# GpSimd's share of the first stage from chunk 6 on given to VectorE, and the sum of the flags taken in the second stage

## The chip, the cores and the metric

The kernel runs on one NeuronCore of a Trainium2 chip. Its time is the device time of one execution in microseconds (us), as the median of several runs. In the rows of the profile the engines are called PE (TensorE, with PEld for its weight loads), DVE (VectorE), ACT (ScalarE), POOL (GpSimd) and SP (SyncE, whose queue issues the DMAs).

## The reference

The program is a complex-decay linear attention followed by two feed-forward blocks, all in float32.

```python
def _attn_ref(q, k, v, a_re, a_im):            # (B, H, S, D) = (4, 8, 768, 48)
    mag = np.sqrt(a_re * a_re + a_im * a_im)
    scale = np.minimum(mag, 0.999) / (mag + 1e-06)
    a_re_n, a_im_n = (a_re * scale, a_im * scale)
    for t in range(S):
        ar, ai = (a_re_n[:, :, t, :, None], a_im_n[:, :, t, :, None])
        new_re = ar * S_re - ai * S_im
        new_im = ar * S_im + ai * S_re
        S_re, S_im = (new_re + einsum('bhd,bhe->bhde', k_t, v_t), new_im)
        y[:, :, t] = einsum('bhd,bhde->bhe', q_t, S_re)
    return y

x = attention output as (3072 tokens, 384)
x = (1 / (1 + exp(-(x @ w_gate))) * (x @ w_val)) @ w_out      # d_ff 1536
h = x @ w_in;  out = (h - tanh(h)) @ w_out2                   # d_ff 2048
```

## The kernel before

The 3072 tokens are cut into 24 chunks of 128. For each chunk the decays' angles and magnitudes are computed (functions `theta`, `phase`, `sincos`, `magnitude`), q and k are multiplied by them, and the attention within the chunk and the state passed on to the next are done with small matmuls (`pe_units`). Two chunks make a block of 256 tokens, and the first feed-forward block runs over the 12 blocks, 12 slices of the hidden dimension each: two products on TensorE into a PSUM tile `gv` (line 888), the gate on ScalarE (896) and VectorE (903), the result split into a high and a low part (ScalarE 911, VectorE 912), and three steps later the product back into `acc` (935). That is the first stage; the attention of the chunks to come is woven into it. The second stage (from about 713 us of the span) runs the second feed-forward block over six groups of 512 tokens: `hstep` (1070), `cubic` on ScalarE and VectorE, `split2` (1082, 1083) and `fin` (1096).

Each float32 product that needs it is made of three products of a rounded high part and a difference. The weights of the second block are decoded and split while the first stage runs: `Decoder.tick` (line 289) loads a raw slice, ScalarE and VectorE make the value `sg` (lines 64, 66, 72, 75), `split` (320) lets ScalarE write the high part (323) and the engine in `low` the difference (325), and SyncE stores both in DRAM (327). There are 32 such slices. `low` is POOL alone in the kernel before.

`shared(c, k)` (line 442) says which engine does the elementwise product number `k` of chunk `c`. From chunk 6 on POOL does numbers 9 and 10, k times the inverse suffix of the magnitudes (`suf`, line 566) and q times their running product (`B`, line 567); VectorE does the rest. `suf` comes from a scan on VectorE (549), followed there by `whole` (554, four columns) and the scan for `B` (562). The products feed `stack` (584, 586, 590), and this the scores (716), the transposes of k (728, copied by ScalarE in 729) and the states (781).

Late in the first stage `late_within` tests the decays of the first six chunks again for the flags (424 to 426). `open2` (1017) calls `flag_sum` (978): a maximum over the flags on VectorE (980), a product with a column of ones on TensorE (984), a copy (985). A flag above zero would send the program to a general path; with these inputs it is not taken.

What sets the order: the functions are called in an order given by `merge` and `until`; SyncE's queue keeps that order as written, and the instructions of the other engines are put in order by a scheduler that plans with its own estimates of durations. Each engine then runs its list strictly in order, so an instruction that waits holds all behind it. PSUM tiles come from pools of a few buffers: `pat` with three for the attention, `P2["h"]` with three for `h` in the second stage and `h4` with one more for every fourth step.

Of the kernel before, what the change touches and what calls it, by code (L numbers as in the profile page):

```python
# [8 lines left out]
F32 = mybir.dt.float32  # L9
# [12 lines left out]
NF1, NF2 = FF1 // 128, FF2 // 128  # L22
# [24 lines left out]
POOLED = ((9, 10), (3, 4, 9, 10), (3, 4, 6, 10), (2, 3, 4, 6, 9, 10, 11), (3, 4, 5), (10,))  # L47
# [3 lines left out]
EARLY = 6  # L51
# [192 lines left out]
def kernel(ctx: ExitStack, tc: tile.TileContext, ri, qk, vv, w1, w2, out):  # L244
    nc = tc.nc
    w1i = w1.bitcast(I32)
    w2i = w2.bitcast(I32)
# [18 lines left out]
    pat = att.enter_context(tc.tile_pool(name="pat", bufs=3, space=PSUM, side="right"))  # L266
# [72 lines left out]
    for f in range(NF1):  # L339
        for p in range(2):  # L340
            n = 2 * f + p
# [98 lines left out]
        return load, test  # L440

    def shared(c, k):
        return nc.gpsimd if (k in POOLED[c] if c < EARLY else k in (9, 10)) else nc.vector

    def theta(c):

# [23 lines left out]
        def t2():  # L470
            A, C, R = d["A"], d["C"], d["R"]
            shared(c, 2).tensor_tensor(R, A, C, ALU.add)
# [51 lines left out]
    def magnitude(c):  # L524
# [39 lines left out]
        def m5():  # L564
            Q, K = qkt[c][:, 0], qkt[c][:, 1]
            shared(c, 9).tensor_tensor(K, K, suf, ALU.mult)  # L566
            shared(c, 10).tensor_tensor(Q, Q, d["B"], ALU.mult)
# [376 lines left out]
    def moe1(units, extra):  # L944
# [8 lines left out]
        for n, (j, f, cols) in enumerate(order):  # L953
            if n == last:
                run_to(until[n])
                open2()
            dec1.ready(min(3 * f + 4, 36) if j == 0 and cols is A else 36 if j > 1 else 0)
            gv(n)
            if n >= 1:
                split(n - 1)  # L960
            run_to((until[n] + until[n + 1]) / 2)
            extra(2 * (n - last) + 1)
            if n >= LAG1:
                outp(n - LAG1)
                jo, fo, co = order[n - LAG1]
                if jo == 0 and co is Z:
                    dec1.part(fo, 2, gated[n - 1])
            if n == last - (NB - 3) * NF1 + LAG1:
                early.close()
                gvp[2] = ph1.enter_context(tc.tile_pool(name="pgv2", bufs=1, space=PSUM))  # L970
            gate(n)
            if j == 0 and cols is Z:
                dec1.part(f, 0, gated[n])
                dec1.part(f, 1, gated[n])
            run_to(until[n + 1])
            extra(2 * (n - last) + 2)

    def flag_sum():
        fs = const.tile([RB, 1], F32, name="fs")
        nc.vector.tensor_reduce(fs, flags, mybir.AxisListType.X, ALU.max)  # L980
        one = const.tile([RB, 1], F32, name="one")
        nc.vector.memset(one, 1.0)
        fp = pat.tile([1, 1], F32, tag="at", name="fp")
        nc.tensor.matmul(fp, fs, one)
        nc.vector.tensor_copy(fsum.bitcast(F32), fp)

    with tc.manual_schedule(engines={mybir.EngineType.SP}):
# [27 lines left out]
        P2, W2 = {}, {}  # L1015

        def open2():
            flag_sum()
            att.close()
            P2["x0"] = ph2.enter_context(tc.tile_pool(name="m2x", bufs=1, side="right"))  # L1020
            P2["xr"] = ph2.enter_context(tc.tile_pool(name="m2r", bufs=2, side="right"))
            P2["h"] = ph2.enter_context(tc.tile_pool(name="p2h", bufs=3, space=PSUM, side="right"))
            P2["t"] = ph2.enter_context(tc.tile_pool(name="m2t", bufs=2, side="right"))
            P2["g"] = ph2.enter_context(tc.tile_pool(name="m2g", bufs=3, side="right"))

        w2d = [dram.tile([128, 2, 384], F32, name=f"w2d{s}") for s in range(2 * NF2)]
        dec2 = Decoder(w2i, NF2, 2, ring0, lambda s: 2, (nc.gpsimd,), w2d)

        def load_w2(upto):
            while len(W2) < min(upto, 2 * NF2):  # L1030
                s = len(W2)
                hl = wp.tile([128, 2, 384], F32R, tag=f"w{SLOT[s // 3, s % 3]}", name="whl")
                nc.sync.dma_start(out=hl.bitcast(F32), in_=w2d[s])
                W2[s // 2, s % 2] = hl
# [4 lines left out]
        def load_x2(i, z):  # L1039
            if z == 0:  # L1040
                x2t[i] = P2[f"x{i % 2}"].tile([128, 2, 2, 3, N1], F32R, tag="x2h", name="x2h")
            hl = x2t[i]
            r = P2["xr"].tile([128, 3, N1], F32, tag="x2r", name="x2r")
            nc.sync.dma_start(out=r, in_=x2d[2 * i + z])
            nc.scalar.copy(hl[:, 0, z], r)
            nc.vector.tensor_tensor(hl[:, 1, z], r, hl[:, 0, z].bitcast(F32), ALU.subtract)
# [14 lines left out]
        def hstep(n):  # L1061
            i, f = divmod(n, NF2)
            x = x2t[i]
            ps = P2["h" if n % 4 < 3 else "h4"].tile([128, N2], F32, tag="h", name="h")
            w = W2[f, 0]
            k = 0
            for kt in range(3):
                cs = slice(kt * 128, (kt + 1) * 128)
                for wi, xi in ((0, 0), (0, 1), (1, 0)):
                    nc.tensor.matmul(ps.rearrange("p (z c) -> p z c", z=2), w[:, wi, cs], x[:, xi, :, kt],  # L1070
                                     start=(k == 0), stop=(k == 8))
                    k += 1
            hps[n] = ps

        def cubic(n):
            prev = (lambda: split2(n - 1)) if n else None
            gt2[n] = cubic_rest(nc, P2["t"], hps.pop(n), N2, prev)

        def split2(n):
            g = gt2[n]  # L1080
            gh = P2["g" if n % 4 < 3 else "g4"].tile([128, 2, N2], F32R, tag="gh2", name="gh2")
            nc.scalar.copy(gh[:, 0], g)  # L1082
            nc.vector.tensor_tensor(gh[:, 1], g, gh[:, 0].bitcast(F32), ALU.subtract)  # L1083
            gt2[n] = gh

        def fin(n):
            i, f = divmod(n, NF2)
            gh = gt2.pop(n)
            if f == 0:
                acc2[i] = [P2["acc"].tile([128, DM], F32, tag=f"o{t}", name=f"o{t}") for t in range(4)]  # L1090
            a = acc2[i]
            w = W2[f, 1]
            for t in range(4):
                cs = slice(t * 128, (t + 1) * 128)
                for k, (gi, wi) in enumerate(((0, 0), (0, 1), (1, 0))):
                    nc.tensor.matmul(a[t], gh[:, gi, cs], w[:, wi], start=(f == 0 and k == 0),  # L1096
                                     stop=(f == NF2 - 1 and k == 2), skip_group_check=True)
                if f == NF2 - 1:
                    ob = P2["o"].tile([128, DM], F32, tag="ob", name="ob")
                    if True:  # L1100
                        nc.scalar.copy(ob, a[t])
                    else:
                        nc.vector.tensor_copy(ob, a[t])
                    r0 = i * N2 + t * 128
                    nc.sync.dma_start(out=out[r0:r0 + 128, :], in_=ob)
# [19 lines left out]
        for n in range(LAG2, total + LAG2):  # L1125
            i, f = divmod(n, NF2)
            if n < total:
                load_w2(32)
                hstep(n)
            if n == total:  # L1130
                split2(n - 1)
            if f in (6, 8) and i + 1 < NT // N2:
                load_x2(i + 1, f // 2 - 3)
            if (n - LAG2) % NF2 == NF2 - 1:
                fin(n - LAG2)
            if n < total:
                cubic(n)
            if (n - LAG2) % NF2 != NF2 - 1:
                fin(n - LAG2)
# [66 lines left out]
```

## Time and profile before

| what | value |
|---|---|
| median of 3 runs | 1128.53 us (1127.44 to 1130.26) |
| the profiled execution | 1129.34 us, its span 1127.6 us |
| granted TensorE clock, mean over the span | 0.986 |
| PE busy | 1050.3 us, 93% |
| DVE busy | 885.4 us, 79% |
| ACT busy | 829.3 us, 74% |
| POOL busy | 158.4 us, 14% |
| DMA | 100.21 MB, mean 89 GB/s |

The span is the time from the first to the last instruction; 1.7 us of the execution lie around it. Busy time is the sum of stretches in which the engine had an instruction under way. Between two instructions an engine is idle, and the profile names what ended the idle time. Since all engines run in order, the chain of waits is read from TensorE backwards.

### The profile page before, as it was taken

How to read it: one execution, taken by the hardware profiler on the slowest of the kernel's cores; microseconds unless marked ns; L12 is line 12 of the kernel's file. 1: busy time of each engine (PE TensorE's matmuls, PEld its weight loads, DVE VectorE, ACT ScalarE, POOL GpSimd, SP SyncE). 2: the span in 40 equal slices, each digit the busy share in tenths (PEclk: the TensorE clock that was granted, in tenths of full speed). 3: DMA queues.
4: the chain of work that ended last, by engine and by line, in shares of the span. 5: the costliest groups of instructions: out<-in, count | busy, mean ns of one | idle time of the engine just before them, and what ended most of it. 6: DMA issues, size and time to landing. Idle time of an engine off the chain costs nothing.

```text
span 1127.6 us, 22170 instructions
## 1 busy us (share of the span) xinstructions
PE 1050.3 (93%) x8782; PEld 982.3 (87%) x8782; DVE 885.4 (79%) x1475; ACT 829.3 (74%) x1828; POOL 158.4 (14%) x126
## 2 busy tenths in 40 slices
PE   0597999999999999998999999999999999999996
PEld 0486899899999999997998989999998989999996
DVE  6899885987778798989998743587878788787875
ACT  8698785887878897977988573566767676676764
POOL 2335431011001212122213200000000000000000
PEclk9998999999999999999999999999999999999999
DMA  6356003122112344453344446700101010010000
GB/s 228 129 196 190 29 18 88 36 71 74 46 59 60 129 141 133 136 181 104 124 157 123 154 150 246 259 1 1 56 1 56 1 56 2 1 57 1 28 1 31
DMA packets 36400, 100.21 MB, mean 89 GB/s; under 512 B 4128, under 2 KB 7200, under 8 KB 36288
## 3 DMA queue, kind: packets, MB, share of 16 engines
q1 hardware_dynamic: 36288, 98.71, 26.7%
q8 instruction: 71, 1.16, 0.4%
q14 instruction: 41, 0.34, 0.1%
HBM read 76.68 MB, written 22.02 MB: 88 GB/s over the span
## 4 chain that ended last, share of the span: by engine, by line
PE 64%; DVE 13%; ACT 13%; DMA 6%; issue 3%; POOL 1%; SPq 0%; DVEq 0%; ACTq 0%; POOLq 0%
PE h L1070 18%; PE o L1096 17%; PE gv L888 14%; PE acc L935 7%; DMA ri<-in_ri_dram 3%; DMA raw<-in_w_dram 2%; PE gv L884 2%; PE xps L751 2%; PE sc L716 1%; ACT raw L64 1%; DVE suf L549 1%; ACT raw L66 1%; PE gps L781 1%; DVE gh L912 1%; DVE sg L75 1%
## 5 line engine op out<-in xcount | busy, mean ns | idle before, releaser
L888 PE MATMUL gv<-x,whl 128*128 128x256 f32 x2376 | 314.6, 286 | 3.2 <-ACT x L602 2.6
L888 PEld LDWEIGHTS gv<-x,whl 128*128 128x128 f32 x2376 | 295.4, 192 | 8.4 <-issue 3.4
L1096 PE MATMUL o<-whl,gh 128*128 128x384 f32 x1152 | 216.6, 337 | 0.6 <-ACT gh L1082 0.6
L1070 PE MATMUL h<-x2h,whl 128*128 128x512 f32 x864 | 216.0, 394 | 0.0
L1096 PEld LDWEIGHTS o<-whl,gh 128*128 128x128 f32 x1152 | 203.6, 188 | 9.3 <-ACT gh L1082 0.9
L1070 PEld LDWEIGHTS h<-x2h,whl 128*128 128x128 f32 x864 | 160.9, 188 | 29.9
L935 PE MATMUL acc<-gh,whl 128*128 128x256 f32 x1188 | 174.3, 290 | 2.5 <-DVE gh L912 2.2
L935 PEld LDWEIGHTS acc<-gh,whl 128*128 128x128 f32 x1188 | 153.1, 192 | 7.2 <-DVE gh L912 3.1
L89 ACT ACTIVATE s<-h 128x512 f32<-128x512 f32 x96 | 57.8, 602 | 114.5 <-PE h L1070 114.4
L1083 DVE TENSOR_TENSOR gh<-g,gh 128x512 fp32r<-128x512 f32 x96 | 66.3, 690 | 43.8 <-ACT gh L1082 43.5
L912 DVE TENSOR_TENSOR gh<-g,gh 128x256 fp32r<-128x256 f32 x132 | 73.9, 561 | 30.3 <-ACT gh L911 29.2
L97 DVE TENSOR_TENSOR th<-h,th 128x512 f32<-128x512 f32 x96 | 66.4, 691 | 31.6 <-ACT th L95 30.7
L896 ACT ACTIVATE th<-gv 128x256 f32<-128x256 f32 (+1 forms) x156 | 56.3, 361 | 38.8 <-PE gv L888 30.4
L903 DVE SCALAR_TENSOR_TENSOR g<-th,gv 128x256 f32<-128x256 f32 x132 | 54.3, 413 | 37.8 <-ACT th L896 36.7
L98 DVE COPY_PREDICATED g<-mk,th 128x512 f32<-128x512 int32 x96 | 72.3, 754 | 1.0
L911 ACT CAST gh<-g 128x256 fp32r<-128x256 f32 x132 | 52.8, 401 | 26.2 <-DVE g L903 25.7
L91 DVE SCALAR_TENSOR_TENSOR g<-g,s 128x512 f32<-128x512 f32 x96 | 65.5, 682 | 3.3 <-ACT g L90 3.3
L1082 ACT CAST gh<-g 128x512 fp32r<-128x512 f32 x96 | 59.2, 617 | 11.3 <-DVE g L98 11.0
L92 DVE TENSOR_TENSOR g<-g,h 128x512 f32<-128x512 f32 x96 | 65.0, 678 | 3.1
L566 POOL TENSOR_TENSOR qk<-qk,suf 112x512 f32<-112x512 f32 x21 | 31.2, 1484 | 253.3 <-DMA qk<-in_qk_dram 102.4
L325 POOL TENSOR_TENSOR raw<-sg,raw 128x384 fp32r<-128x384 f32 x32 | 40.6, 1269 | 166.7 <-ACT raw L323 129.1
L96 ACT ACTIVATE mk<-s 128x512 f32<-128x512 f32 x96 | 60.8, 633 | 0.0
(165 smaller groups left out, 1697.5 us busy)
## 6 DMA issues: line engine op xcount, KB each, us to landing
raw<-in_w_dram SPq DMA_DIRECT2D x68, 384.0 KB, 5.1
ri<-in_ri_dram SPq DMA_DIRECT2D x30, 448.0 KB, 5.3
w2d<-raw SPq DMA_DIRECT2D x32, 384.0 KB, 4.1
whl<-w2d SPq DMA_DIRECT2D x32, 384.0 KB, 5.0
qk<-in_qk_dram SPq DMA_DIRECT2D x24, 448.0 KB, 4.9
v<-in_vv_dram SPq DMA_DIRECT2D x24, 320.0 KB, 3.5
x2d<-x SPq DMA_DIRECT2D x12, 384.0 KB, 2.3
x2r<-x2d SPq DMA_DIRECT2D x12, 384.0 KB, 3.7
```

The source lines that it names most:

```text
L91: nc.vector.scalar_tensor_tensor(g, g, TC * TB, s, ALU.add, ALU.mult)
L92: nc.vector.tensor_tensor(g, g, ps, ALU.mult)
L96: nc.scalar.activation(mk, s, AF.Relu, bias=-0.0625)
L97: nc.vector.tensor_tensor(th, ps, th, ALU.subtract)
L98: nc.vector.copy_predicated(g, mk.bitcast(I32), th)
L888: nc.tensor.matmul(ps[:, part], w[:, wi, cs], x[:, xi, kt], start=(k == 0), stop=(k == 8))
L912: nc.vector.tensor_tensor(gh[:, 1], g, gh[:, 0].bitcast(F32), ALU.subtract)
L935: nc.tensor.matmul(o, w[:, wi, cs], gh[:, gi], start=(f == 0 and k == 0 and (m == 0 or m == 2 and not half)), stop=(f == NF1 - 1 and k == ...
L1070: nc.tensor.matmul(ps.rearrange("p (z c) -> p z c", z=2), w[:, wi, cs], x[:, xi, :, kt], start=(k == 0), stop=(k == 8))
L1082: nc.scalar.copy(gh[:, 0], g)
L1083: nc.vector.tensor_tensor(gh[:, 1], g, gh[:, 0].bitcast(F32), ALU.subtract)
L1096: nc.tensor.matmul(a[t], gh[:, gi, cs], w[:, wi], start=(f == 0 and k == 0), stop=(f == NF2 - 1 and k == 2), skip_group_check=True)
```

## The change

There are three edits. `shared` gives the products 9 and 10 of the chunks from 6 on to VectorE. The decoder of the second block's weights takes VectorE for the differences. `flag_sum` is no longer called in `open2` but after the step `n == 16` of the second stage, and its PSUM tile is a piece of a tile of the pool for `h` instead of one of `pat`.

```diff
     def shared(c, k):
-        return nc.gpsimd if (k in POOLED[c] if c < EARLY else k in (9, 10)) else nc.vector
+        return nc.gpsimd if c < EARLY and k in POOLED[c] else nc.vector
...
-        fp = pat.tile([1, 1], F32, tag="at", name="fp")
+        fp = P2["h"].tile([128, 512], F32, tag="h", name="fp")[0:1, 0:1]
         nc.tensor.matmul(fp, fs, one)
         nc.vector.tensor_copy(fsum.bitcast(F32), fp)
...
         def open2():
-            flag_sum()
             att.close()
...
-        dec2 = Decoder(w2i, NF2, 2, ring0, lambda s: 2, (nc.gpsimd,), w2d)
+        dec2 = Decoder(w2i, NF2, 2, ring0, lambda s: 2, (nc.vector,), w2d)
...
                 hstep(n)
+                if n == NF2:
+                    flag_sum()
```

The scheduler makes a new order from this. On VectorE, around the second scan of chunk 19 (in `magnitude`), the list before reads as follows; L590 is the last product of `stack`, for which the scores wait.

```order
L544 SCALAR_TENSOR_TENSOR B<-A,B 112x512
L545 SCALAR_TENSOR_TENSOR A<-C,B 112x512
L549 SCALAR_TENSOR_TENSOR suf<-A,sufs 112x511
L552 RECIPROCAL pseed<-suf 112x4
L554 TENSOR_TENSOR whole_118<-suf,A 112x4
L562 SCALAR_TENSOR_TENSOR B<-A,pseed 112x512
L590 TENSOR_TENSOR qs<-qk,ri 48x4x128
L912 TENSOR_TENSOR gh<-g,gh 128x256
L903 SCALAR_TENSOR_TENSOR g<-th,gv 128x256
```

The same place of VectorE's list in the changed kernel:

```order
L590 TENSOR_TENSOR qs<-qk,ri 48x4x128
L325 TENSOR_TENSOR raw<-sg,raw 128x384
L545 SCALAR_TENSOR_TENSOR A<-C,B 112x512
L912 TENSOR_TENSOR gh<-g,gh 128x256
L903 SCALAR_TENSOR_TENSOR g<-th,gv 128x256
L549 SCALAR_TENSOR_TENSOR suf<-A,sufs 112x511
L552 RECIPROCAL pseed<-suf 112x4
L554 TENSOR_TENSOR whole_118<-suf,A 112x4
L566 TENSOR_TENSOR qk<-qk,suf 112x512
L562 SCALAR_TENSOR_TENSOR B<-A,pseed 112x512
L72 SCALAR_TENSOR_TENSOR sg<-raw 128x384
L912 TENSOR_TENSOR gh<-g,gh 128x256
```

L590 has moved ahead of both scans, a difference L325 stands behind it, the product L566 stands between `whole` and the second scan, and the product L567 is the next row after the last one shown.

On TensorE, where the first block's last slices begin, the list before has the product of the flags between two steps:

```order
L935 MATMUL acc_8304<-gh,whl 128x256 x6
L935 MATMUL acc_8305<-gh,whl 128x256 x3
L984 MATMUL fp<-one,fs 1x1
L888 MATMUL gv<-x,whl 128x256 x18
L935 MATMUL acc_8304<-gh,whl 128x256 x6
```

In the changed kernel that place has no such row, and the product stands in the second stage, after step 16 of `hstep` (L1069 and L1095 are lines 1070 and 1096 of the kernel before):

```order
L1095 MATMUL o_9458<-whl,gh_9832 128x384 x2
L1095 MATMUL o_9459<-whl,gh_9832 128x384 x3
L1069 MATMUL h<-x2h,whl 128x512 x5
L984 MATMUL fp<-one,fs 1x1
L1095 MATMUL o_9456<-whl,gh_9869 128x384 x2
```

It now follows the last of step 16's products instead of the last `acc` products before the new block's `gv`. The maximum over the flags on VectorE (L980) stays where it was.

## Rows read from the trace of the kernel before

**Rows 1.** Waits of TensorE from 160 us on: total us, times, longest.

```profile
PE gps L781 <- ACT kt L729: 6.8, 7, 2.1
PE gv L888 <- ACT x L602: 2.6, 2, 1.4
PE acc L935 <- DVE gh L912: 2.2, 3, 1.5
PE sc L716 <- DVE qs L590: 2.0, 1, 2.0
PE fp L984 <- DVE fs L980: 0.8, 1, 0.8
```

**Rows 2.** Stretches 240:440 and 440:640: length, then PE, PEld, DVE, ACT, POOL busy.

```profile
240.00:440.00 200.00, 200.00 (x2147) 192.75 (x2146) 160.86 (x292) 160.11 (x389) 33.28 (x24) 1.00 0.29 92
...
440.00:640.00 200.00, 189.18 (x2034) 181.77 (x2033) 179.80 (x302) 166.54 (x402) 46.78 (x35) 0.99 0.41 132
```

**Rows 3.** POOL's groups in 440:640: busy us, mean ns, idle before them.

```profile
L325 POOL TENSOR_TENSOR raw<-sg,raw 128x384 fp32r<-128x384 f32 x21 | 26.5, 1262 | 88.7 <-ACT raw L323 68.2 <-DMA qk<-in_qk_dram 13.9 <-issue 5.4
L567 POOL TENSOR_TENSOR qk<-qk,B 112x512 f32<-112x512 f32 x7 | 10.3, 1468 | 4.0 <-DVE B L562 4.0
L566 POOL TENSOR_TENSOR qk<-qk,suf 112x512 f32<-112x512 f32 x7 | 10.3, 1466 | 55.4 <-DMA qk<-in_qk_dram 23.0 <-DVE suf L549 20.4 <-DVE whole L554 11.9
```

**Rows 4.** Three of VectorE's groups in 440:640, same columns.

```profile
L912 DVE TENSOR_TENSOR gh<-g,gh 128x256 fp32r<-128x256 f32 x45 | 29.0, 645 | 6.4 <-ACT gh L911 5.8
L75 DVE SCALAR_TENSOR_TENSOR sg<-raw,sg 128x384 int32<-128x384 int32 x21 | 16.2, 771 | 0.4
L554 DVE TENSOR_TENSOR whole<-suf,A 112x4 f32<-112x4 f32 x7 | 5.3, 753 | 0.0
```

**Rows 5.** Single lines over the whole span: ns min/median/max, first and last start.

```profile
L912 DVE TENSOR_TENSOR gh<-g,gh x132: 389/425/2467, 141.7 to 713.4; 128x256 fp32r<-128x256 f32 x132
L75 DVE SCALAR_TENSOR_TENSOR sg<-raw,sg x32: 544/558/1646, 360.3 to 658.9; 128x384 int32<-128x384 int32 x32
L554 DVE TENSOR_TENSOR whole<-suf,A x24: 127/152/2244, 22.9 to 622.6; 112x4 f32<-112x4 f32 x24
L317 DVE TENSOR_TENSOR whl<-whole,whl x18: 526/554/1455, 82.0 to 171.5; 128x384 fp32r<-128x384 f32 x18
L566 DVE TENSOR_TENSOR qk<-qk,suf x3: 677/682/686, 63.0 to 145.7; 112x512 f32<-112x512 f32 x3
```

**Rows 6.** VectorE in order of time around chunk 19: start, us, instruction.

```profile
512.29 2.24 DVE L554 TENSOR_TENSOR whole<-suf,A 112x4 f32<-112x4 f32 x1
514.46 1.21 DVE L562 TENSOR_TENSOR_SCAN B<-A,pseed 112x512 f32<-112x512 f32 x1
515.70 0.69 DVE L590 TENSOR_TENSOR qs<-qk,ri 48x512 f32<-48x512 f32 x1
516.42 1.38 DVE L912 TENSOR_TENSOR gh<-g,gh 128x256 fp32r<-128x256 f32 x1
```

**Rows 7.** POOL in order of time, same stretch.

```profile
512.24 1.30 POOL L566 TENSOR_TENSOR qk<-qk,suf 112x512 f32<-112x512 f32 x1 [11.09 <-DVE suf L549]
513.50 1.01 POOL L325 TENSOR_TENSOR raw<-sg,raw 128x384 fp32r<-128x384 f32 x1
515.75 1.77 POOL L567 TENSOR_TENSOR qk<-qk,B 112x512 f32<-112x512 f32 x1 [1.23 <-DVE B L562]
```

**Rows 8.** Longest wait of ScalarE in 430:640.

```profile
ACT raw L323 <- DVE sg L75: 11.3, 7, 3.3
```

**Rows 9.** TensorE in order of time where the last block begins.

```profile
671.94 0.19 PE L984 MATMUL fp<-one,fs 112*1 112x1 f32 x2 [0.82 <-DVE fs L980]
673.48 0.38 PE L888 MATMUL gv<-x,whl 128*128 128x256 f32 x1 [1.36 <-ACT x L602]
```

**Rows 10.** SyncE's waits for POOL's differences, whole span.

```profile
SPq L327 <- POOL raw L325: 44.1, 8, 9.8
```

**Rows 11.** ScalarE's first step of `cubic` and what it waited for.

```profile
L89 ACT ACTIVATE s<-h 128x512 f32<-128x512 f32 x96 | 57.8, 602 | 114.5 <-PE h L1070 114.4
```

## The prediction

> **What bounds the kernel now.** I read the page first: PE is busy 93% of the span and carries 64% of the chain that ended last, so only time in which TensorE stands still can be won. Then the waits of TensorE from 160 us on, where the start-up is over: the five largest come to 6.8 + 2.6 + 2.2 + 2.0 + 0.8 = 14.4 us [rows 1]. That is nearly all an edit of this kind can move, 1.3% of the time. The busy times by stretch say where these waits lie: from 240 to 440 us TensorE never pauses (200.00 of 200.00 us) and VectorE is busy 160.86, but from 440 to 640 us, where the decoding of the second block's weights runs as well, VectorE is busy 179.80 and TensorE 189.18, so 10.8 us of its waits are there [rows 2]. The reader is to see that VectorE, with 20.2 us to spare in 200, is the tightest helper in just the stretch where TensorE waits.
>
> Last I read what VectorE does there instruction by instruction. The product for `whole` has four columns and takes 0.15 us in the median, but 2.24 us at 512.29 [rows 5, 6]. It runs exactly while POOL's L566 (1.30 us) and L325 (1.01 us) do, and ends when they end; L912 (median 0.425 us) takes 1.38 us beside POOL's L567 [rows 5 to 7]. So a POOL product holds up the VectorE product that meets it.
>
> One rule bears on the sum. The Trainium skill (SBUF — State Buffer, Who interferes with whom) says that GpSimd and a VectorE instruction with two SBUF inputs compete for one read interface, and the later one stands still until the earlier has finished; the 2.24 us agree with that. If every POOL product in the stretch held VectorE for its whole length, 26.5 + 10.3 + 10.3 = 47.1 us of VectorE's time would come back there [rows 3], and VectorE would have 25.8 us less to do than now; the measured stretch, below, is less than half of this, and the sum goes by it.
>
> **The change part by part.**
>
> *The products given to VectorE.* From 440 to 640 us these are 21 differences L325 and 7 + 7 products of q and k [rows 3]. On VectorE a difference of 128x384 takes 0.55 us (the same form in L317) and a product of 112x512 takes 0.68 us [rows 5]. That adds 21 x 0.55 + 14 x 0.68 = 21.1 us.
>
> *The blocking that goes.* For the three groups that show it most, mean less median, times count [rows 4, 5]: L912 (0.645 - 0.425) x 45 = 9.9; L75 (0.771 - 0.558) x 21 = 4.5; L554 (0.753 - 0.152) x 7 = 4.2. Together 18.6 us, a lower bound, since the smaller groups are left out. VectorE's load therefore becomes at most 179.8 + 21.1 - 18.6 = 182.3 us of 200. As a load the edit is a wash; 17.7 us stay free, and from 240 to 440 us, with 39 us free and no wait of TensorE, the products are hidden whole.
>
> *What the wash is worth to TensorE.* It is not one everywhere. Where POOL's products came in a bunch, they held VectorE for a time the scheduler had not planned. I work one place: around chunk 19 blocking cost 2.24 - 0.15 = 2.1 us in `whole` and 1.38 - 0.43 = 0.95 us in L912 [rows 5, 6]; the new list puts one product (0.68 us) between `whole` and the second scan, and L567 behind L912. Up to L912, that is 3.05 us given back for 0.68 paid. Elsewhere POOL's products met nothing that they could block, and there VectorE now pays in full.
> Term by term:
> - Scores waiting for L590: 2.0 us [rows 1]. L590 stood behind the blocked `whole` and the scan; in the new list it stands ahead of both scans. What is late next there is the mask and then L912, both with less ahead of them. Taken as gone: 2.0 (ends 0 and 2.0; the order decides it).
> - States waiting for ScalarE's copy of the transposed k: 6.8 us in seven waits. ScalarE is late there because it waited itself: 11.3 us in seven waits for VectorE's L75 [rows 8], one of the blocked groups. Bounds 0 (VectorE's load is a wash) and 6.8. I take half, 3.4, since the place worked above gives back more than it pays but the load as a whole does not.
> - `acc` waiting for VectorE's L912: 2.2 us in three, the longest 1.5. L912 is the line with most blocking, but one product now stands ahead of it. Bounds 0 and 2.2; I take 0.8, a third, as only one of the three (after the L912 of 1.38 us) is worked out.
> - `gv` waiting for ScalarE's L602: 2.6 us in two. The one of 1.36 us is at the last block [rows 9]: ScalarE's tests of the flags stand ahead of its L602 and stay there. Of the other 1.2 us I take half, 0.6.
> - The flags' product on TensorE waits 0.82 us, and right after it TensorE waits 1.36 us for L602 [rows 9]. With the product gone it would wait for L602 from the start, so nothing is won: 0, bounds 0 and 0.8 + 0.2.
>
> Against these 2.0 + 3.4 + 0.8 + 0.6 = 6.8 us stands the part of the added load that is not given back, 21.1 - 18.6 = 2.5 us; I put all of it on the path (bounds 0 and 21.1).
>
> *The flags' product in the second stage* costs TensorE 0.2 us there as it did before [rows 9]. Its tile takes one turn of the three buffers for `h`, so step 18 waits for the reading of step 16 instead of step 14. Between the two lie a full step 17 and a row of `fin`, and ScalarE waits 114.4 us in all for `h`, that is, it stands ready when a step ends [rows 11]. Hidden; 1 to 2 us if VectorE is late just there.
>
> *DMAs.* SyncE's list is unchanged, but each store of a slice now waits for VectorE's L325 instead of POOL's, where it waited 44.1 us in all [rows 10]. A later store makes the loads behind it later. POOL's products of q and k mostly waited for their own load [rows 3], so what comes later has some room; I cost it at nothing, and 1 us per place if that cover is gone.
>
> Sum: 6.8 - 2.5 = 4.3 us. From the profiled execution, 1129.34 us, this gives 1125.0; the median of the runs lies 0.8 us under that execution, so the forecast for the median is 1124.2 us. About 3.4 us (0.3%) is what can be told from no change, so the forecast is faster by little more than that.
>
> **The rivals.**
>
> *The wash is a wash (1127.8).* VectorE's time is the same, ScalarE stays late and only the score wait goes. For it: the sum of rows, +21.1 against 18.6, and ScalarE's 166.54 us of 200 are untouched. Against it: the blocking came in bursts. Then 2.0 us are won and half of the 2.5 us lost, so 0.75 us: 1129.34 - 0.8 - 0.75 = 1127.8. The Trainium skill (Perfetto Trace Analysis, Optimizing Scalar/DVE Operations) says of the two engines that, as they share a read port, moving work between them "might not help"; by this the time would be that of before, and the loads in these rows agree with it.
>
> *All waits of the tight stretch go (1116.5).* If the scheduler's plan, in which nothing is blocked, is now kept on the chip, TensorE runs from 440 to 640 as it does from 240 to 440: 6.8 + 2.0 + 2.2 + 1.2 = 12.2 us less, with the extra load in VectorE's 17.7 free us. For it: not one wait where VectorE has 39 us free. Against it: VectorE stays nearly as full as it is.
>
> *VectorE takes over POOL's waits (1133.7).* POOL idled 68.2 us for ScalarE's L323 before the differences and 36.9 us for q and k's load [rows 3]; that cost nothing, as nothing stood behind it. On VectorE the gates L903 and L912 stand behind each such wait. VectorE has 17.7 us left for 35 products, so the point from which it decides is a mean wait of 0.5 us. At 0.65 us, 5.2 us go on the path: 1129.34 - 0.8 + 5.2 = 1133.7. For it: the lists are strictly in order. Against it: the new list puts the products behind scans and gates (L325 behind L590, L566 behind `whole`), later than POOL began them.
>
> **How the numbers follow.** Forecast 0.48, with its own range 1121 to 1127.5; wash 0.24; all waits gone 0.17; VectorE bound 0.11. Of the forecast's range two thirds lie under 1125.1, so faster is 0.17 + 0.32 = 0.49; slower is 0.10, most of the last rival; the rest, 0.41, is within 0.3%. The range of 8 in 10 goes from 1117.5, close to the second rival's time, to 1130, short of the third.
>
> **What would show it.** Right: no POOL product from chunk 6 on; `whole` at 0.15 us throughout and L912 near 0.43 us in the mean; VectorE's busy time from 440 to 640 between 176 and 184 us; no wait of the scores for L590; the waits for L729 about half. Wrong: VectorE idle before L325 or L566 by more than 0.5 us each (third rival), waits of the states as before (first), or TensorE without a pause from 440 to 640 (second). A pause of TensorE at step 18 of the second stage would show the tile's turn not hidden.

## The result, and the profile after

The changed kernel takes 1112.05 us in the median of 6 runs (1108.2 to 1112.92), the kernel before 1128.06 us beside it (6 runs, 1124.94 to 1130.26): a ratio of 0.9851, with an interval of 0.9832 to 0.987. That is 16 us less, nearly four times the forecast gain, and below the forecast range. The profiled execution took 1112.92 us, its span 1111.2 us, against 1127.6 us before.

The busy times of the whole span come first (the page's first part: busy us, share, instructions).

```profile
PE 1047.5 (94%) x8782; PEld 980.8 (88%) x8782; DVE 881.0 (79%) x1543; ACT 829.5 (75%) x1828; POOL 65.8 (6%) x58
```

VectorE took over 68 products and is busy for less time than before, 881.0 against 885.4 us. TensorE's waits from 160 us on (total us, times, longest) answer to [rows 1]:

```profile
PE xps L651 <- DVE pt L622: 1.1, 2, 0.8
PE gps L781 <- ACT kt L729: 0.7, 3, 0.3
PE acc L935 <- DVE gh L912: 0.7, 2, 0.4
PE o L1095 <- ACT gh L1081: 0.6, 1, 0.6
```

Of the five that were listed before, 14.4 us, there are 1.4 left (kt and `acc`); one of 1.1 us is new. The waits for L590, for L602 and for the flags are gone. The two stretches, with the columns of [rows 2]:

```profile
240.00:440.00 200.00, 199.84 (x2149) 192.73 (x2148) 166.47 (x318) 161.42 (x392) 0.00 (x0) 1.00 0.29 92
...
440.00:640.00 200.00, 199.29 (x2154) 193.13 (x2153) 176.25 (x351) 178.15 (x432) 0.00 (x0) 1.00 0.45 147
```

From 440 to 640 us TensorE is busy 10.1 us longer than before, 199.29 of 200 us, so the stretch runs like the one ahead of it. VectorE is busy 3.6 us less there while it does the products of POOL as well, and it runs 351 instructions where it ran 302. The groups of VectorE in 440:640 (busy us, mean ns, idle before them) answer to [rows 3, 4]:

```profile
L912 DVE TENSOR_TENSOR gh<-g,gh 128x256 fp32r<-128x256 f32 x47 | 19.6, 418 | 7.1 <-ACT gh L911 7.0
L75 DVE SCALAR_TENSOR_TENSOR sg<-raw,sg 128x384 int32<-128x384 int32 x23 | 12.7, 553 | 0.1
L325 DVE TENSOR_TENSOR raw<-sg,raw 128x384 fp32r<-128x384 f32 x23 | 12.6, 552 | 0.9 <-ACT raw L323 0.8
L566 DVE TENSOR_TENSOR qk<-qk,suf 112x512 f32<-112x512 f32 x7 | 4.8, 686 | 0.0
L567 DVE TENSOR_TENSOR qk<-qk,B 112x512 f32<-112x512 f32 x7 | 4.8, 686 | 0.0
L554 DVE TENSOR_TENSOR whole<-suf,A 112x4 f32<-112x4 f32 x7 | 1.0, 137 | 0.0
```

L912 fell from 645 to 418 ns in the mean, `whole` from 753 to 137 ns, L75 from 771 to 553 ns. The products that VectorE took over cost what was said (0.55 and 0.69 us), and VectorE hardly waits for their operands. The place around chunk 19, VectorE in order of time (start, us), answers to [rows 6, 7]:

```profile
511.67 0.14 DVE L554 TENSOR_TENSOR whole<-suf,A 112x4 f32<-112x4 f32 x1
511.73 0.69 DVE L566 TENSOR_TENSOR qk<-qk,suf 112x512 f32<-112x512 f32 x1
512.33 1.22 DVE L562 TENSOR_TENSOR_SCAN B<-A,pseed 112x512 f32<-112x512 f32 x1
...
513.91 0.42 DVE L912 TENSOR_TENSOR gh<-g,gh 128x256 fp32r<-128x256 f32 x1
514.25 0.69 DVE L567 TENSOR_TENSOR qk<-qk,B 112x512 f32<-112x512 f32 x1
```

The scan for `B` starts 0.66 us after `whole`; before it was 2.17 us. ScalarE's wait for L75 in 430:640, against [rows 8]:

```profile
ACT raw L323 <- DVE sg L75: 2.1, 3, 1.1
```

It was 11.3 us in seven waits. ScalarE is busy 178.15 us in 440 to 640, 11.6 us more than before, since more of its work falls into that stretch.

Where the 16.4 us of the span went: from 440 to 680 us TensorE's busy time rose from 226.37 to 239.29 us (the same view of both kernels), so 12.9 us of standing still are gone there; TensorE's busy time over the whole span is 2.8 us less; the remaining 0.7 us lie in the other stretches.

Part of the shorter busy time is the clock. In the kernel before, TensorE stood still for 2.13 us at 605 us, and right behind this its granted clock was at the lower level (1.2 GHz) for a time. The stretch 600:620 of the kernel before and of the changed one (the third figure from the end is the mean granted clock as a share of the full 2.4 GHz):

```profile
600.00:620.00 20.00, 17.87 (x205) 17.00 (x205) 16.98 (x31) 19.34 (x45) 4.16 (x3) 0.91 0.26 84
...
600.00:620.00 20.00, 20.00 (x219) 19.61 (x208) 19.84 (x41) 16.63 (x42) 0.00 (x0) 1.00 0.39 120
```

Three rows of TensorE in order of time there, before; nine products of L935 take 2.27 us behind the wait and 1.34 us a little later:

```profile
607.08 0.67 PE L781 MATMUL gps<-v,kt 128*64 128x48 f32 x16 [2.13 <-ACT kt L729]
...
608.87 2.27 PE L935 MATMUL acc<-gh,whl 128*128 128x256 f32 x9
...
615.91 1.34 PE L935 MATMUL acc<-gh,whl 128*128 128x256 f32 x9
```

From the two clocks, (1.00 - 0.91) x 20 us, an estimate of 1.8 us of TensorE's time was lost so before, and none after. So this wait cost more than its own length.

### The profile page after: what moved, and what is told of

Read it like the earlier page. It is cut to its first block, busy times and chain, and to the rows that moved or that the text cites. A ratio compares the mean times of both kernels' runs of the same rounds, so it can differ in the third digit from the quotient of the medians.

```text
span 1111.2 us, 22084 instructions
## 1 busy us (share of the span) xinstructions
PE 1047.5 (94%) x8782; PEld 980.8 (88%) x8782; DVE 881.0 (79%) x1543; ACT 829.5 (75%) x1828; POOL 65.8 (6%) x58
## 4 chain that ended last, share of the span: by engine, by line
PE 64%; ACT 14%; DVE 12%; DMA 7%; issue 3%; SPq 0%; POOL 0%; ACTq 0%; DVEq 0%; POOLq 0%
PE h L1069 18%; PE o L1095 18%; PE gv L888 14%; PE acc L935 7%; DMA ri<-in_ri_dram 5%; PE xps L751 2%; PE gv L884 2%; DMA raw<-in_w_dram 1%; PE sc L716 1%; ACT raw L64 1%; PE gps L781 1%; DVE whole L72 1%; ACT raw L66 1%; DVE suf L549 1%; ACT L510 1%
## 5 line engine op out<-in xcount | busy, mean ns | idle before, releaser
L1095 PE MATMUL o<-whl,gh 128*128 128x384 f32 x1152 | 216.6, 337 | 0.6 <-ACT gh L1081 0.6
L1069 PE MATMUL h<-x2h,whl 128*128 128x512 f32 x864 | 216.0, 394 | 0.0
L1095 PEld LDWEIGHTS o<-whl,gh 128*128 128x128 f32 x1152 | 203.4, 188 | 9.3 <-ACT gh L1081 0.9
L1069 PEld LDWEIGHTS h<-x2h,whl 128*128 128x128 f32 x864 | 160.9, 188 | 29.9
L935 PE MATMUL acc<-gh,whl 128*128 128x256 f32 x1188 | 172.0, 288 | 0.8 <-DVE gh L912 0.7
L935 PEld LDWEIGHTS acc<-gh,whl 128*128 128x128 f32 x1188 | 151.9, 191 | 4.7 <-DVE gh L912 1.1
L903 DVE SCALAR_TENSOR_TENSOR g<-th,gv 128x256 f32<-128x256 f32 x132 | 54.6, 415 | 34.2 <-ACT th L896 33.5
L912 DVE TENSOR_TENSOR gh<-g,gh 128x256 fp32r<-128x256 f32 x132 | 56.3, 428 | 22.2 <-ACT gh L911 20.9
L90 ACT ACTIVATE g<-s 128x512 f32<-128x512 f32 x96 | 60.5, 630 | 0.1
L95 ACT ACTIVATE th<-h 128x512 f32<-128x512 f32 x96 | 56.8, 592 | 3.6 <-DVE g L92 3.6
```

Of the source, the lines that this page charges most:

```text
L90: nc.scalar.activation(g, s, AF.Square, scale=math.sqrt(TC), bias=math.sqrt(TC) * TA)
L935: nc.tensor.matmul(o, w[:, wi, cs], gh[:, gi], start=(f == 0 and k == 0 and (m == 0 or m == 2 and not half)), stop=(f == NF1 - 1 and k == ...
```

## The experiments

Two theories stood against each other at first. Theory A: POOL's products hold VectorE up, the scheduler's order doesn't count it, and the chip falls behind that order. Theory B: the products came late because POOL is slow at them. Theory C put the gain down to the sum of the flags. Each ratio is to the kernel before on the same chip; the medians of that kernel were 1127.0 to 1128.6 us.

**VectorE does the products of q and k alone** (of the change, this edit only):

```diff
-        return nc.gpsimd if (k in POOLED[c] if c < EARLY else k in (9, 10)) else nc.vector
+        return nc.gpsimd if c < EARLY and k in POOLED[c] else nc.vector
```

> One part alone: VectorE does q and k times their decays from chunk 6 on; the differences of w2 stay on POOL and the flags' sum stays in the first stage. Theory A (POOL's products hold up VectorE unplanned, and all of the gain is that): the two kinds of products held VectorE about equally from chunk 6 on, so about half the gain of 16 us comes, 6 to 10 us, 1118 to 1122 us. Theory B (the gain is in q and k being ready sooner, 0.68 us on VectorE for 1.47 us on POOL): nearly all of it, 1112 to 1115 us. Theory C (the gain is the flags' sum leaving the seam between the last blocks): none, 1127 to 1129 us.

Measured: 1113.35 us, 0.9891 [0.9867, 0.9916]. That is what theory B gave, and more gain than the half that theory A gave.

**VectorE does the differences of w2 alone:**

```diff
-        dec2 = Decoder(w2i, NF2, 2, ring0, lambda s: 2, (nc.gpsimd,), w2d)
+        dec2 = Decoder(w2i, NF2, 2, ring0, lambda s: 2, (nc.vector,), w2d)
```

> One part alone: VectorE writes the differences of w2; q and k times their decays stay on POOL, the flags' sum stays in the first stage. Theory A: about half the gain, 1118 to 1122 us. Theory B: none or a loss, 1126 to 1132 us. Theory C: none, 1127 to 1129 us.

Measured: 1117.26 us, 0.9925 [0.9897, 0.9954]. Either edit alone takes more than half of the gain: by the medians beside them 13.7 and 9.8 us of the 17.6 for both. Theory B expected nothing of this edit; theory A expected two halves and missed both numbers, with more gain than it gave. These two runs alone do not decide between them. The stretch 440:640 of both, the products of q and k first:

```profile
440.00:640.00 200.00, 196.60 (x2126) 189.85 (x2125) 174.36 (x322) 173.73 (x426) 28.47 (x23) 1.00 0.45 145
```

```profile
440.00:640.00 200.00, 193.90 (x2092) 187.08 (x2091) 180.44 (x332) 173.13 (x420) 22.22 (x14) 0.99 0.42 138
```

In the second, with POOL's 14 products of q and k left, the states still wait for the copy of k:

```profile
PE gps L781 <- ACT kt L729: 6.3, 5, 2.0
```

**The flags' sum in the second stage alone:**

```diff
-        fp = pat.tile([1, 1], F32, tag="at", name="fp")
+        fp = P2["h"].tile([128, 512], F32, tag="h", name="fp")[0:1, 0:1]
...
-            flag_sum()
...
+                if n == NF2:
+                    flag_sum()
```

> One part alone: the flags' sum is taken in the second stage; POOL keeps its products. Theories A and B: at most the 0.8 us that TensorE waited for the maximum, so 1127 to 1129 us. Theory C: TensorE's 2.4 us at the seam and more, 1113 to 1126 us.

Measured: 1127.18 us, 1.002 [0.9998, 1.0041]. Theory C falls. Its trace shows the trade that the prediction gave: the wait for the flags is gone, and at the last block TensorE waits for L602 from the start (start, us, instruction, idle before it):

```profile
669.93 0.38 PE L888 MATMUL gv<-x,whl 128*128 128x256 f32 x1 [2.22 <-ACT x L602]
```

It is the 0.82 + 1.36 = 2.18 us of [rows 9] in one piece.

**Both products on VectorE, the flags' sum left in the first stage** (the changed kernel with the edit just shown undone):

> The change without its third part: VectorE has both kinds of products, the flags' sum stays in the first stage. Theories A and B: as the whole change, 1111 to 1114 us, with the wait of 0.8 us for the maximum, and perhaps of 1.4 us for x, still at the seam. Theory C: 1120 us or more.

Measured: 1109.45 us, 0.9859 [0.9835, 0.9884], against 0.9851 for the changed kernel. TensorE's waits from 160 to 760 us are these:

```profile
PE acc L935 <- DVE gh L912: 0.7, 2, 0.4
PE gps L781 <- ACT kt L729: 0.5, 1, 0.5
```

Neither the flags' product nor L602 is among them, although the tests of the flags stand in the first stage as before. So these tests alone do not make ScalarE late at the last block. The time lies a little under the 1111 to 1114 us of theories A and B.

**POOL reads again.** The changed kernel, and behind each of the 68 products that VectorE now does POOL multiplies a dead tile by the same operand; its results are not used.

```diff
+    def echo(dead, x):
+        nc.gpsimd.tensor_tensor(dead, dead, x, ALU.mult)
...
+            echo(w, hl[:, 0].bitcast(F32))
...
+            if c >= EARLY:
+                echo(d["C"], suf)
...
+            if c >= EARLY:
+                echo(d["C"], d["B"])
```

> The changed kernel, and POOL reads again what it read in the kernel before: right behind each product that VectorE now does from chunk 6 on (q and k times their decays, the differences of w2), POOL multiplies a tile that nothing uses any more by the same operand, 36 products of q's and k's size and 32 of w2's. VectorE's own work, and the time at which q, k and w2 are ready, are those of the changed kernel as the scheduler lays it out. Theory A (POOL's products hold VectorE up in a way the scheduler's order doesn't count; that was the whole price): in 440 to 640 us the changed kernel's VectorE is busy for 176 of 200 us, and the blocking that the trace of before shows there is about 25 us, so its products come to 200 of 200 and the time goes back to 1122 to 1140 us. Theory B (q and k, and w2's low parts, came late because POOL is slow at them; the products beside VectorE cost nothing): nothing waits for the repeated products, 1110 to 1114 us.

Measured: 1139.02 us, 1.0089 [1.0071, 1.0108]. Almost nothing waits for these products (VectorE for 0.2 us in the whole span), yet they cost 27 us against the changed kernel and make it slower than the kernel before. Theory B falls. In the trace the instructions of VectorE, ScalarE and TensorE stand in the order of the changed kernel, but for a few that changed places before 200 us, so no new order explains the loss. Stretch 440:640, and TensorE's longest waits from 160 to 760 us:

```profile
440.00:640.00 200.00, 186.50 (x1919) 179.10 (x1919) 191.91 (x331) 165.25 (x396) 49.28 (x35) 0.97 0.40 131
```

```profile
PE gps L789 <- ACT kt L737: 11.7, 8, 3.2
PE acc L943 <- DVE gh L920: 3.1, 2, 1.6
PE gv L896 <- DVE g L911: 2.7, 3, 1.4
PE gv L896 <- ACT x L610: 2.5, 2, 1.6
```

Three of the waits of [rows 1] are back (their lines stand 8 lower in this kernel), the first of them with 11.7 us in eight. TensorE's granted clock is 0.97 in the stretch, against 1.00 in the changed kernel, and of the 26.5 us between the two spans 4.9 us are longer busy time of TensorE (1052.4 against 1047.5 us); the other 21.6 us are standing still. The product of k on VectorE (L566 in the changed kernel, 686 ns there) shows the hold-up itself, in the columns of [rows 4]:

```profile
L570 DVE TENSOR_TENSOR qk<-qk,suf 112x512 f32<-112x512 f32 x8 | 10.4, 1300 | 0.0
L558 DVE TENSOR_TENSOR whole<-suf,A 112x4 f32<-112x4 f32 x7 | 6.1, 870 | 0.0
```

**POOL only writes.** The same places, but POOL sets the dead tile to zero twice and reads nothing.

```diff
+    def echo(dead, x):
+        for _ in range(2):
+            nc.gpsimd.memset(dead, 0.0)
```

> Control to the kernel in which POOL reads again: at the same 68 places POOL only writes, it sets the same dead tile to zero twice, and reads nothing. Theory A in its narrow form (it is POOL's reading of two operands that holds VectorE up): 1110 to 1114 us, and VectorE's operations at L912 keep a mean of about 428 ns. Theory A in its wide form (any work of POOL beside VectorE holds it up): 1116 to 1130 us, with L912 well over 450 ns. Theory B: 1110 to 1114 us.

Measured: 1108.88 us, 0.9832 [0.9815, 0.9848]. Stretch 440:640, two of VectorE's groups in it (L912 and L554 in the changed kernel, here 9 and 5 lines lower), then POOL's:

```profile
440.00:640.00 200.00, 199.56 (x2156) 193.61 (x2152) 176.43 (x352) 177.74 (x437) 34.47 (x76) 1.00 0.46 148
```

```profile
L921 DVE TENSOR_TENSOR gh<-g,gh 128x256 fp32r<-128x256 f32 x49 | 20.4, 417 | 7.5 <-ACT gh L920 7.3
L559 DVE TENSOR_TENSOR whole<-suf,A 112x4 f32<-112x4 f32 x7 | 0.9, 135 | 0.0
```

```profile
L276 POOL MEMSET sg<- 128x384 f32 x48 | 20.0, 420 | 125.8 <-DVE raw L329 124.5
L276 POOL MEMSET C<- 112x512 f32 x28 | 14.7, 527 | 46.2 <-DVE A L550 29.7 <-ACT gh L920 9.4 <-ACT th L905 6.0
```

POOL works for 34.7 us beside VectorE, and neither L912's product nor `whole` is longer for it. What holds VectorE up is a POOL product that reads, not POOL's being busy. (POOL is busy for 49.28 us of the stretch where it reads, so the control is the smaller load.) VectorE, ScalarE and TensorE run the lists of the changed kernel here, instruction for instruction: the scheduler laid out the same order whether POOL reads or writes. The 3 us between these two kernels' medians, 1108.88 and 1112.05 us, therefore come of nothing in their orders, and smaller differences between single kernels say little.

**The same products on VectorE.** The echo as above, by `nc.vector`:

```diff
+    def echo(dead, x):
+        nc.vector.tensor_tensor(dead, dead, x, ALU.mult)
```

> The same 68 repeated products as planned work of VectorE instead of POOL, about 36 x 0.68 + 32 x 0.55 = 42 us more for it in all and some 21 to 25 us in 440 to 640 us, where it then is busy for about 198 of 200 us. It tells a load that the scheduler knows of from a hold-up that it doesn't. Theory A (what was lost before was lost because the order was laid out without the hold-up): 1112 to 1122 us, and faster than the kernel in which POOL repeats them. Rival (only the sum of VectorE's occupied time counts, planned or not): as slow as that kernel, within 3 us of it.

Measured: 1115.01 us, 0.9892 [0.9874, 0.991], 24 us faster than with the same 68 products on POOL. Stretch 440:640:

```profile
440.00:640.00 200.00, 198.56 (x2136) 192.41 (x2137) 192.18 (x387) 175.38 (x424) 0.00 (x0) 1.00 0.45 148
```

VectorE is as busy as with POOL's echo (192.18 and 191.91 us), and TensorE is busy for 12.1 us more of the stretch. So VectorE's busy time alone doesn't set the time; the rival, that only its sum counts, falls. The scheduler knew of these products and made another order for them.

**Long pieces on VectorE.** A hold-up came in pieces of up to 2.1 us (`whole`), the echoes above in 0.55 and 0.68 us. To tell this apart:

```diff
+            if c >= EARLY:
+                nc.vector.tensor_reduce(d["C"][:, 0, 0:1], flat(d["B"]).unsqueeze(1).broadcast_to([112, 4, 512]), mybir.AxisListType.XY, ALU.max)
```

> The changed kernel, and behind the product of q of each chunk from 6 on VectorE takes a maximum over four readings of that chunk's B, 112x2048, whose result nothing uses: 18 pieces of an estimated 2.1 us each (four times the 112x512 that a product reads in 0.68 us, without the fixed part of it), about 38 us in all, as much as the 68 repeated products on VectorE but in pieces as long as the hold-ups by POOL were. It tells the length of the pieces from their being unknown to the scheduler. If long pieces cost, known or not: 1122 to 1140 us, like the kernel in which POOL repeats the products. If they cost only where the order was laid out without them: 1112 to 1120 us, like the kernel in which VectorE repeats them (1115).

Measured: 1113.19 us, 0.9868 [0.9843, 0.9893]. The 18 pieces from 160 to 680 us, and the stretch 440:640:

```profile
L569 DVE TENSOR_REDUCE C<-B 112x1 f32<-112x2048 f32 x18 | 41.0, 2276 | 0.0
```

```profile
440.00:640.00 200.00, 199.66 (x2148) 193.82 (x2147) 186.76 (x354) 174.45 (x427) 0.00 (x0) 1.00 0.45 147
```

41.0 us more for VectorE, in pieces of 2.28 us, cost 1 us against the changed kernel and 4 us against the two other kernels with the same products on VectorE (1109.45 and 1108.88 us). The length of a piece that is in the list is not what costs. Here too the order is a new one.

**No product on POOL at all:**

```diff
-POOLED = ((9, 10), (3, 4, 9, 10), (3, 4, 6, 10), (2, 3, 4, 6, 9, 10, 11), (3, 4, 5), (10,))
+POOLED = ((), (), (), (), (), ())
...
-    dec1 = Decoder(w1i, NF1, 3, ring1, lambda s: 6, (nc.vector, nc.gpsimd))
+    dec1 = Decoder(w1i, NF1, 3, ring1, lambda s: 6, (nc.vector,))
```

> The changed kernel carried to its end: POOL does no product at all. The products of chunks 0 to 5 that the kernel's table gives to POOL, and the low parts of w1 that POOL shares with VectorE, are VectorE's too. In the changed kernel POOL is still busy for 65.8 us, nearly all of it before 440 us. Theory A, if it holds there as well: VectorE loses the hold-up and gains the work, about even, so 1106 to 1114 us. Theory B (only the late q, k and w2 mattered) or a VectorE that is full in the first stage: 1113 to 1130 us.

Measured: 1103.64 us, 0.978 [0.9764, 0.9795]. The version beats both kernels. Then **only the second of these two edits** (w1's low parts on VectorE):

> The changed kernel, and in its first stage VectorE alone takes the low parts of w1, of which POOL took every other one; POOL keeps the products of chunks 0 to 5. It tells where the further gain of the kernel without any product on POOL (8.4 us against the changed kernel, 1103.6 against 1112.05) comes from. If the low parts of w1 hold VectorE up as those of w2 did: 1105 to 1109 us, with the rest from the products of the chunks. If that gain is from the chunks' products alone: 1110 to 1113 us.

Measured: 1105.45 us, 0.9794 [0.9772, 0.9817], so w1's low parts bring the larger part of the further gain. And **no product on POOL, the flags' sum in the first stage:**

> No product on POOL anywhere, and the sum of the flags back in the first stage, as in the kernel before. The kernel with VectorE's products alone and the sum in the first stage came out at 1109.45 us, the changed kernel, which moves the sum to the second stage, at 1112.05 us, in different calls. If the move of the sum costs about 2 us: 1100 to 1102.5 us here. If it costs nothing: 1102.5 to 1105 us, as the kernel without products on POOL that has the sum in the second stage.

Measured: 1103.51 us, 0.9784 [0.9761, 0.9806]: moving the sum costs nothing and brings nothing. The start-up, 0:160, of the version without products on POOL:

```profile
0.00:160.00 160.00, 113.46 (x1186) 103.02 (x1186) 142.18 (x280) 136.22 (x297) 4.96 (x19) 0.96 0.44 139
```

In the changed kernel TensorE is busy 107.78 us there, at a mean granted clock of 0.91; the kernel in which POOL only writes, with the same lists, has 0.95 there. Over the whole span the version's TensorE is busy 1043.7 us against 1047.5, and stands still 6.2 us less. Whether the clock or the work comes first there was not tried. Against the kernel in which POOL only writes, the gain of this version is 5.2 us in the medians, against the changed kernel 8.4 us, so its size is not settled.

**The held time against the time.** The trace gives the hold-up from chunk 6 on: for each VectorE instruction that is under way beside a product of POOL, its length less the median of the same instruction with none beside it. The work is what VectorE has to do beyond the kernel before, by 0.68 us a product, 0.55 us a difference and, in the last row, the 41.0 us shown. The flags' sum alone stands here with the kernel before, since its products are on POOL too.

| kernel | held, us | added work, us | both | time, us |
|---|---|---|---|---|
| before | 38.2 | 0 | 38 | 1128.06 |
| flags' sum alone | 36.4 | 0 | 36 | 1127.18 |
| q and k on VectorE | 14.3 | 24.5 | 39 | 1113.35 |
| w2 on VectorE | 23.2 | 17.6 | 41 | 1117.26 |
| changed kernel | 0 | 42.1 | 42 | 1112.05 |
| both products, flags early | 0 | 42.1 | 42 | 1109.45 |
| POOL only writes | 0 | 42.1 | 42 | 1108.88 |
| POOL reads again | 47.4 | 42.1 | 90 | 1139.02 |
| VectorE repeats | 0 | 84.2 | 84 | 1115.01 |
| long pieces | 0 | 83.1 | 83 | 1113.19 |

The sum of both columns orders nothing: seven kernels with 36 to 42 us lie 19 us apart, three with 83 to 90 us lie 26 us apart. The held time orders them, down to 14.3 us; the five kernels with none lie between 1108.88 and 1115.01 us, and the row with 14.3 us among them. Five of these kernels, the first four rows among them, ran beside one another on one chip: there, against the 1109.45 us of the one with both products on VectorE, 14.3 us of held time cost 3.9 us, 23.2 us cost 7.8 us and 38.2 us (1127.03 us there) cost 17.6 us. So the two edits' gains overlap: while the hold-ups are few, the slack of the engines takes up more of them.

The scheduler's order doesn't count the hold-ups: it is the same with POOL reading as with POOL writing, but for those few before 200 us, and the times of these two kernels are 30 us apart. Work that is in its list cost 1 to 6 us for 41 to 42 us, long or short. An order laid out with the hold-ups counted was not tried, nor the order of the kernel before without them; how much of the loss a better order would save, and how the 16 us divide between the hold-ups and the new order, is open.

## Why the prediction was wrong, step by step

- *What bounds the kernel, and where.* Right: TensorE's waits of 440 to 640 us are what went. The 14.4 us as "nearly all an edit of this kind can move" were a little too few: 16.4 us came off the span, 2.8 of them from TensorE's busy time. The prediction had no term for that; an estimated 1.8 us of it is the lower clock behind the wait at 605 us, which went with the wait.
- *The products on VectorE, 21.1 us.* Right in price (0.55 and 0.69 us each). VectorE's busy time in the stretch, 176.25 us, lies at the bottom of the 176 to 184 given.
- *The blocking that goes, 18.6 us.* Right in kind, short in size: counted for all groups it is 24.9 us there, so the edit gives back 3.6 us more than it takes where 2.5 us less were put on the path. This is 6 us of VectorE's time, and it mattered little: 41.0 us more of planned work cost 1 to 4 us.
- *"What the wash is worth to TensorE".* This is the step that failed. It priced the hold-ups as load, so that a wash of loads halved the waits. Two kernels with VectorE busy 192 of 200 us, one held up and one not, came out 24 us apart. The terms that rest on it fell short together: the states' wait went from 6.8 to 0.7 us and not to half; `acc` from 2.2 to 0.7 us and not to 1.4; and the 2.5 us "all on the path" had no place in the sum. Of the listed waits 13.0 us went where 6.8 were forecast. These 6.2 us, the 2.5 us and the 2.8 us of busy time are 11.5 of the 12.1 us by which the forecast gain of 4.3 us fell short of the 16.4 us of the span.
- *The wait for L602 at the last block (1.36 us) stays.* Wrong: with both products on VectorE it is gone whether the flags are summed in the first stage or in the second, so the tests of the flags alone are not its cause. It comes back where VectorE gets more to do, 1.59 us in the kernel that repeats the products on VectorE and 2.51 us in that with the long pieces, so at this one place VectorE's load, or the order made for it, still matters.
- *The scores' 2.0 us.* Right, gone; with the products of q and k alone on VectorE 1.3 us of it are left, so it took the differences too.
- *The flags' sum: nothing won in the first stage, nothing lost in the second.* Right: 1.002 [0.9998, 1.0041] alone, and no wait at step 18. ScalarE's wait for `h` is unchanged, against [rows 11]:

```profile
L89 ACT ACTIVATE s<-h 128x512 f32<-128x512 f32 x96 | 57.8, 602 | 114.3 <-PE h L1069 114.2
```

- *DMAs at nothing.* Right. SyncE's wait for the differences, against [rows 10], is shorter:

```profile
SPq L327 <- DVE raw L325: 25.6, 5, 9.8
```

- *The rivals.* "All waits of the tight stretch go" came nearest: by it the scheduler's plan is kept on the chip and these waits go. It gave 12.2 us (its time should then read 1116.3 and not 1116.5 us); the waits at the last block (2.2 us) and TensorE's shorter busy time (2.8 us) come on top of it. It got 0.17 because VectorE "stays nearly as full as it is"; the kernel in which VectorE repeats the products shows that fullness was no argument. "VectorE takes over POOL's waits" fell: L566 and L567 waited 0.0 us in the stretch and L325 0.9 us in 23, far below 0.5 us each.
- *A slip.* If POOL held VectorE for the whole length of its products, VectorE would have 47.1 - 21.1 = 26.0 us less to do, not 25.8. Nothing in the sum goes by it.

The Trainium skill (SBUF — State Buffer, Who interferes with whom) says that a VectorE instruction with two SBUF inputs contends with a GpSimd instruction that reads SBUF, and not with one that only writes it. The runs agree: 1139.02 us with POOL reading, 1108.88 us with POOL only writing. In the trace of before L903, which reads `gv` in PSUM, takes 410 ns in the mean in 22 places beside a POOL product and 413 ns elsewhere, while L912 takes 920 ns in 36 and 418 ns. The Trainium skill's remark that moving work between the two engines "might not help" (Perfetto Trace Analysis, Optimizing Scalar/DVE Operations), which the first rival named, is not borne out here: 0.9851.

## What to carry to other kernels

Time for which one engine holds up another is not a load to be netted against the work moved: here 42 us of useless work in the scheduler's list cost 3 to 6 us, and 47 us of hold-ups, in an order that didn't count them, cost 27 to 30 us. That such a stop passes down each queue behind it is the likely reason, not a shown one. Where one engine is held at a few lines (min and median short, maximum long) and another engine waits for the held one, price the edit by the waits that chain back to those stops. Before moving work off an engine that is nearly full, or onto it, test the fullness by giving it useless work of the same size. And when kernels are only a few us apart, look at TensorE's granted clock in each before a cause is given.

## What the runs showed of the hardware that was not expected

A POOL product did not hold VectorE for its whole length: in the kernel before POOL's products from 160 us on are 40.6 + 25.9 + 25.3 = 91.8 us, and VectorE was held for 38.2 us. The scans are held too: with POOL doing only q and k, the scan for `B` takes 1.64 us in the mean in 6 places beside a POOL product and 1.22 us in the other 12. Small work can be held longest: `whole`, four columns, went from 0.15 to 2.24 us.
